# Folding a convolution through DRAM, moving products from VectorE to ScalarE and GpSimd, and a longer search for the instruction order

## The chip, the cores and the metric

The kernel runs on one core of a Trainium2 chip. The metric is device microseconds from start to end of one execution. Three executions of the kernel before took 842.36, 843.04 and 845.2 us; their median is 843.04 us. One further execution was recorded by the hardware profiler. Engines are called by the profile's names: PE is TensorE's matmul, PEld its weight load, DVE is VectorE, ACT is ScalarE, POOL is GpSimd, SP is SyncE (it issues DMAs).

## The reference

There are 4 batches. Each has an attention over 8 heads of 576 positions and 64 dimensions, in which every query keeps only its 32 largest scores, then two feed-forward blocks.

```python
scores = scale * np.matmul(q, k.transpose(0, 1, 3, 2))
kth = np.partition(scores, -32, axis=-1)[..., -32:-31]
scores = np.where(scores >= kth, scores, -1000000000.0)
attn = np.exp(scores - max);  attn = attn / (np.sum(attn) + 1e-09)
x = np.matmul(attn, v)                       # heads side by side: 576 x 512
# block 1
h = np.maximum(x @ w_in, 0.0);  u, v = h[..., :512], h[..., 512:]
v_n = (v - mean(v)) / np.sqrt(var(v) + 1e-06)
v_s = np.einsum('ts,bsd->btd', w_spatial, v_n) + b_spatial[None, :, None]
x = (u * v_s) @ w_out
# block 2: a causal convolution of 5 taps, each channel with its own taps
for k in range(5):
    gate_pre += conv_w[k][None, None, :] * xp[:, k:k + S, :]
out = ((1.0 / (1.0 + np.exp(-gate_pre))) * (x @ w_val)) @ w_out2
```

## The kernel before, in words

The work is cut into units. A unit is two tiles of 128 queries; a batch has 18 units, the program 72. For each unit PE makes the scores (`scores`, L475), ACT copies them from PSUM to the tile `sb` (L478), and DVE finds the 32nd largest of each row (`top`, L494 to L529): maxima and minima of halves and quarters give a list of candidates, and four rounds of an 8-fold maximum, with the found values replaced in between, walk down it. ACT takes the exponentials (L521). DVE multiplies them by the mask and sums them (`mask`, L546). ACT adds 1e-9 to the two sums (L550), DVE takes the reciprocal (L551), ACT scales the rows by it (L554). PE transposes them (L563, L568) and multiplies them by v (L584).

The two feed-forward blocks ("MoE") of batch b run beside the attention of batch b+1; those of batch 3 run alone after the last unit and are called the tail here. Their matrix products are kept near float32 by writing each operand as a high and a low part in the type fp32r and adding three products (`mm3`, L625). `hilo` (L604) makes the parts: ACT rounds the high part (L609), POOL subtracts it from the value for the low part (L611). In order, a batch has the pieces `piece_v` and `piece_u` (w_in), `piece_sp` (the product with w_spatial on PE, L728, then u times it on DVE, L733), `piece_x2` (w_out), `conv`, `piece_val` (w_val, then the gate times it on DVE, L805) and `piece_out`. Columns (positions) are worked in two halves of 288 and channels in four blocks of 128, so `piece_sp`, `conv` and `piece_val` each come 8 times a batch.

For batches 0 to 2 the convolution runs on PE: for each tap a 128x128 diagonal matrix of the coefficients, again in high and low parts, is multiplied with the shifted columns, 15 matmuls to a piece (L777). The 40 diagonals are built by ACT (L291). For batch 3 DVE does it by four multiply-adds a piece (L788). Since sigmoid(y) is (1 + tanh(y/2))/2, ACT makes the tanh (L780, L791) and DVE adds 1 while it multiplies by val (L805).

Weights come as 64-bit floats and are decoded at the start (`decode`, L305), written to DRAM and loaded again, 2 MB at a time, by DMAs that POOL issues (L403).

Nothing is issued in the order of the source. Every piece of work is recorded with its engine, an assumed duration and what it reads and writes (`Order.add`); `Order.play` then simulates a list schedule with these durations, and `Order.plan` plays it forward and back for 4 rounds and keeps the order with the shortest played time. That order is the program order of each engine, and each engine then issues strictly in that order: an instruction that waits holds up all that stand behind it on its engine.

Buffers that matter below: three PSUM banks `mp` for the MoE pieces while attention runs, three `sb`, two `e`, six `gate`.

## Time and profile before

| | before |
|---|---|
| median of three runs | 843.04 us |
| the profiled execution's own time | 839.99 us |
| its span, first to last instruction | 838.1 us |
| busy: PE, DVE, ACT, POOL | 708.3, 754.7, 602.8, 290.6 us |
| mean granted TensorE clock | 0.922 of full speed |

Busy time is the union of an engine's instructions; an instruction's duration includes a start and an end that overlap its neighbours, so in a dense stretch the time from one start to the next is what an instruction costs, and it is less than the mean that the profile prints. An fp32 matmul of the program (not a transpose, and not fp32r) is recorded as two. DVE's last instruction of attention ends at 742 us; the rest of the span is the tail.

### The profile page before, as it was taken

How to read it: one execution, taken by the hardware profiler on the slowest of the kernel's cores; microseconds unless marked ns; L12 is line 12 of the kernel's file. 1: busy time of each engine (PE TensorE's matmuls, PEld its weight loads, DVE VectorE, ACT ScalarE, POOL GpSimd, SP SyncE). 2: the span in 40 equal slices, each digit the busy share in tenths (PEclk: the TensorE clock that was granted, in tenths of full speed). 3: DMA queues.
4: the chain of work that ended last, by engine and by line, in shares of the span. 5: the costliest groups of instructions: out<-in, count | busy, mean ns of one | idle time of the engine just before them, and what ended most of it. 6: DMA issues, size and time to landing. Idle time of an engine off the chain costs nothing.

```text
span 838.1 us, 17270 instructions
## 1 busy us (share of the span) xinstructions
PE 708.3 (85%) x5969; PEld 605.2 (72%) x5969; DVE 754.7 (90%) x2749; ACT 602.8 (72%) x1390; POOL 290.6 (35%) x353
## 2 busy tenths in 40 slices
PE   3245545755899999998999999997999999999986
PEld 2234433544789899876888899875888999778985
DVE  6999999999999999999999999998989999951580
ACT  5668866777887777768977777786886777774341
POOL 4767255564523311132442322232333112322120
PEclk9955666777999999999999999998999999999999
DMA  7888332323134502153133412234035003533601
GB/s 248 245 261 304 101 121 91 115 86 109 39 100 146 184 2 76 55 196 120 29 134 113 156 30 102 100 101 143 2 142 194 23 2 131 210 120 123 221 2 61
DMA packets 46954, 99.25 MB, mean 118 GB/s; under 512 B 22532, under 2 KB 29960, under 8 KB 43272
## 3 DMA queue, kind: packets, MB, share of 16 engines
q0 software_dynamic: 4032, 53.74, 18.1%
q1 hardware_dynamic: 42824, 44.31, 16.8%
q8 instruction: 49, 0.80, 0.4%
q14 instruction: 49, 0.40, 0.2%
HBM read 79.88 MB, written 18.15 MB: 117 GB/s over the span
## 4 chain that ended last, share of the span: by engine, by line
DVE 51%; PE 23%; ACT 6%; issue 2%; POOL 1%; DMA 0%; POOLq 0%; DVEq 0%; ACTq 0%
DVE tw L527 10%; DVE e L546 10%; PE mp L625 8%; DVE t8b L529 7%; PE mp L728 4%; DVE tm L494 4%; DVE cand L503 4%; DVE tm L495 3%; DVE cand L506 3%; PE xr L584 3%; DVE t8a L516 2%; DVE cand L498 2%; PE sps L475 2%; DVE tn L499 2%; DVE gate L788 2%
## 5 line engine op out<-in xcount | busy, mean ns | idle before, releaser
L475 PE MATMUL sps<-k,q 64*128 64x144 f32 (+1 forms) x1280 | 126.4, 341 | 85.2 <-ACT sb L478 77.9
L475 PEld LDWEIGHTS sps<-k,q 64*128 64x128 f32 (+1 forms) x1280 | 90.4, 201 | 116.0 <-ACT sb L478 88.6
L546 DVE SCALAR_TENSOR_TENSOR e<-sb,t8b,e 128x576 f32<-128x576 f32 x144 | 132.5, 945 | 0.1
L529 DVE MAX8 t8b<-tw 128x8 f32<-128x168 f32 x432 | 120.3, 318 | 0.0
L554 ACT ACTIVATE e<-e,sums 128x576 f32<-128x576 f32 x144 | 106.6, 770 | 9.5 <-DVE sums L551 9.3
L521 ACT ACTIVATE e<-sb,neg 128x576 f32<-128x576 f32 x144 | 106.5, 770 | 2.2 <-PE ptp L563 1.0
L478 ACT ACTIVATE sb<-sps 128x576 f32<-128x576 f32 x144 | 93.0, 646 | 19.6 <-PE sps L475 17.2
L563 PE MATMUL ptp<-ident,e 128*128 128x128 f32 x576 | 94.5, 301 | 11.1 <-ACT e L554 8.5
L584 PE MATMUL xr<-pt,vt 128*64 128x128 f32 (+1 forms) x1280 | 87.8, 281 | 18.0 <-ACT pr L570 17.7
L625 PE MATMUL mp<-xh,wblk 128*128 128x288 f32 x448 | 102.2, 306 | 0.0
L584 PEld LDWEIGHTS xr<-pt,vt 128*64 128x64 f32 x1280 | 68.3, 144 | 36.4 <-ACT pr L570 23.6
L563 PEld LDWEIGHTS ptp<-ident,e 128*128 128x128 f32 x576 | 72.0, 153 | 25.0 <-ACT e L554 13.1
L527 DVE MATCH_REPLACE8 tw<-t8b,tw 128x168 f32<-128x168 f32 x288 | 88.8, 314 | 0.0
L565 ACT ACTIVATE pt<-ptp 128x512 f32<-128x512 f32 x144 | 81.7, 596 | 8.4 <-PE ptp L563 8.1
L625 PEld LDWEIGHTS mp<-xh,wblk 128*128 128x128 f32 x448 | 74.6, 188 | 5.5 <-issue 1.2
L625 PE MATMUL mp<-wblk,xh 128*128 128x512 f32 (+1 forms) x280 | 73.9, 406 | 1.1 <-POOL stage L327 1.1
L494 DVE TENSOR_TENSOR tm<-sb 128x576 f32<-128x576 f32 x72 | 58.8, 817 | 5.6 <-ACT sb L478 5.4
L611 POOL TENSOR_TENSOR yl<-ux,yh 128x288 fp32r<-128x288 f32 x31 | 29.5, 953 | 94.9 <-ACT yh L609 92.5
L625 PE MATMUL mp<-xl,wblk 128*128 128x288 f32 x224 | 60.9, 294 | 0.0
L625 PEld LDWEIGHTS mp<-wblk,xh 128*128 128x128 f32 (+1 forms) x280 | 49.8, 186 | 14.9 <-POOL stage L327 1.3
L495 DVE TENSOR_TENSOR tm<-sb 128x576 f32<-128x576 f32 x72 | 60.4, 838 | 0.0
L503 DVE MAX8 cand<-tm 128x8 f32<-128x288 f32 x144 | 57.8, 441 | 0.0
(180 smaller groups left out, 1687.9 us busy)
## 6 DMA issues: line engine op xcount, KB each, us to landing
wblk<-w_out POOLq DMA_DIRECT2D x7, 2048.0 KB, 8.4
wblk<-w_sp POOLq DMA_DIRECT2D x8, 1440.0 KB, 6.5
wblk<-w_inv POOLq DMA_DIRECT2D x4, 2048.0 KB, 8.3
wblk<-w_inu POOLq DMA_DIRECT2D x4, 2048.0 KB, 9.1
wblk<-w_val POOLq DMA_DIRECT2D x4, 2048.0 KB, 9.0
q<-in_qT SPq DMA_DIRECT2D x16, 288.0 KB, 3.9
k<-in_kT SPq DMA_DIRECT2D x16, 288.0 KB, 4.4
stage<-in_w_in SPq DMA_DIRECT2D x8, 512.0 KB, 4.5
```

Of the source, the lines that this page charges most:

```text
L475: nc.tensor.matmul(dst[:, f:f + QUART], lhsT=l, rhs=r[:, f:f + QUART], start=True, stop=True)
L478: od.add("ACT", t_actp(S), lambda c=c: nc.scalar.activation(sb[:, :, CH[c][0]:CH[c][1]], sps[:, :, 0:HALF], AF.Copy), [("sps",)], [("sb", ...
L494: tt(m[:, :, 0, :], sb[:, :, 0:HALF], sb[:, :, HALF:S], op=ALU.max)
L503: nc.vector.max(cand[:, t, QUART + 16:QUART + 24], m[:, t, 1, :])
L521: od.add("ACT", t_act(S, 1), lambda t=t: nc.scalar.activation(e[:, t, :], sb[:, t, :], AF.Exp, bias=neg[:, t:t + 1], scale=scale), ksb + [ ...
L527: nc.vector.match_replace(w[:, t, :], (t8a if r == 1 else t8b)[:, t, :], (src if r == 1 else w)[:, t, :], LOW)
L529: nc.vector.max(t8b[:, t, :], w[:, t, :])
L546: od.add("DVE", 0.85, lambda t=t, g=g: nc.vector.scalar_tensor_tensor(e[:, t, :], sb[:, t, :], t8b[:, t, 7:8], e[:, t, :], op0=ALU.is_ge, ...
L554: od.add("ACT", t_act(S, 1), lambda t=t, g=g: nc.scalar.activation(e[:, t, :], e[:, t, :], AF.Copy, scale=sums[:, g:g + 1]), [kg[t]], [("e ...
L563: nc.tensor.transpose(pp[:, j, :], e[:, t, REM * t + 128 * j:REM * t + 128 * j + 128], ident)
L584: nc.tensor.matmul(xr[64 * o:64 * o + 64, 2, 0:nq], lhsT=vt[:, kt, 64 * o:64 * o + 64], rhs=r, start=kt == 0, stop=kt == KT - 1)
L625: nc.tensor.matmul(ps, lhsT=l, rhs=r, start=m == 0, stop=m == len(ops) - 1)
```

## The change

1. **Convolution** (batches 0 to 2). `line_out` writes each finished x2 piece (128 channels by 288 columns and 4 more for the taps) to DRAM; four DMAs then read it back "folded" into one of three `fold` tiles: partition 32r+p holds channels p, 32+p, 64+p and 96+p, shifted by r columns. One matmul over the 128 partitions thus sums four taps of 32 channels, and a second one the fifth tap. For the four quarters of the channels that is 8 matmuls in plain fp32, each with 32 output partitions, in place of 15 with 128. Their weights, the tile `band`, are built by 4 POOL instructions after 14 small ACT ones; the 40 diagonals and the tile that held them are gone, and w_out of batch 3 gets a tile of its own (`wlate`) in the place of `band` and `fold`. The coefficients are loaded by 4 DMAs of 32 partitions and decoded at once (80 columns) and not in four jobs (5 columns).
2. **Products** of `piece_sp` and `piece_val` (batches 0 to 2): ACT copies PSUM to one of two `fac` tiles, POOL multiplies. ACT adds 1 to the gate in an instruction of its own.
3. **Sums**: 1e-9 is added on DVE, just ahead of the reciprocal.
4. **Order**: 200 rounds, with noise added to the order that is played back, and a score that is half the played time and half the mean time of three replays with durations lengthened at random by up to 20%. Assumed durations of POOL instructions and of two decode steps are changed as well.

```diff
-    ROUNDS = 4
+    ROUNDS = 200
+    SEED = 1
...
+        def score(run):
+            some = [self.replay(run[2], run[1], f) / 1.1 for f in factors]
+            return 0.5 * run[3] + 0.5 * sum(some) / len(some)
         best = run = self.play(own)
-        for _ in range(self.ROUNDS):
-            ends = [t + self.ops[i][0][e][0] for i, (t, e) in enumerate(zip(run[0], run[1]))]
-            late = self.play(lambda i, e: -ends[i] + (0.0 if first(i, e) else 1e4), back=True)
+        low = score(run)
+        for r in range(self.ROUNDS):
+            spread = 0.0 if r < 4 else rng.choice((0.0, 1.0, 3.0, 8.0))
+            ends = [t + self.ops[i][0][e][0] + spread * rng.gauss(0.0, 1.0) for i, (t, e) in enumerate(zip(run[0], run[1]))]
+            late = self.play(lambda i, e: -ends[i] + (0.0 if e == main[i] else 1e4), back=True)
             by = [late[3] - t - self.ops[i][0][e][0] for i, (t, e) in enumerate(zip(late[0], late[1]))]
-            run = self.play(lambda i, e: by[i] + (0.0 if first(i, e) else self.LATER))
-            best = min(best, run, key=lambda r: r[3])
+            run = self.play(lambda i, e: by[i] + (0.0 if e == main[i] else self.LATER))
+            now = score(run)
+            if now < low:
+                best, low = run, now
+            elif r >= 4:
+                run = best
...
+        NQR, NFOLD, FW = 4, 3, HALF + 1
...
-            flat = cw.rearrange("p k t -> p (k t)")
-            od.add("ACT", 0.2, lambda: nc.scalar.activation(cwp[0], flat, AF.Copy), [("cw",)], [("cwp", 0)], at)
-            od.add("POOL", 0.3, lambda: nc.gpsimd.tensor_tensor(cwp[1], flat, cwp[0].bitcast(F32), op=ALU.subtract),
-                   [("cw",), ("cwp", 0)], [("cwp", 1)], at)
-            for z in range(2):
-                part = cwp[z].bitcast(F32)
-                for d in range(KK):
-                    def go(z=z, d=d, part=part):
-                        for j in range(d * TAPS, (d + 1) * TAPS):
-                            nc.scalar.activation(DIAG[:, z, j, :], ident, AF.Copy, scale=part[:, j:j + 1])
-                    od.add("ACT", TAPS * 0.293, go, [("cwp", z)], [("diag", z, d)], at)
+            quarter = [slice(32 * r, 32 * r + 32) for r in range(4)]
+            def coefs():
+                nc.gpsimd.memset(coef, 0.0)
+                for r, rows in enumerate(quarter):
+                    nc.scalar.activation(cwn[rows], cw[rows, :, r, :], AF.Copy)
+                    nc.scalar.activation(ident4[rows, :], ident[rows, rows], AF.Copy)
+                    nc.scalar.activation(coef[rows, :, :, 0], cw[rows, :, :, r], AF.Copy)
+                nc.scalar.activation(coef[rows, :, :, 1], cw[rows, :, :, 4], AF.Copy)
+            od.add("ACT", 1.6, coefs, [("cw",)], [("cwn",), ("coef",)], at)
+            for d in range(KK):
+                def go(d=d):
+                    n = NQR * 2
+                    nc.gpsimd.tensor_tensor(
+                        BUF["band"][:, d].rearrange("p q m c -> p (q m) c"), ident4.unsqueeze(1).to_broadcast([128, n, 32]),
+                        coef[:, d].rearrange("p q m -> p (q m)").unsqueeze(2).to_broadcast([128, n, 32]), op=ALU.mult)
+                od.add("POOL", 0.8, go, [("coef",), ("cwn",), ("late",)], [("band", d)], at)
...
-            od.add("ACT", 0.2, lambda: nc.scalar.activation(sl, sl, AF.Copy, bias=1e-9), [], kg, ("r", at))
-            od.add("DVE", 0.07, lambda: nc.vector.reciprocal(sl, sl), [], kg, ("r", at))
+            def inverse():
+                nc.vector.tensor_scalar(sl, sl, 1e-9, None, op0=ALU.add)
+                nc.vector.reciprocal(sl, sl)
+            od.add("DVE", 0.135, inverse, [], kg, ("r", at))
...
+            def product(ps, j, x, kx, at):
+                fj = nxt(fa_n, NFAC)
+                od.add("ACT", t_actp(HALF), lambda: nc.scalar.activation(FAC[fj], ps[:, 0:HALF], AF.Copy), [("mp", j)], [("fac", fj)], at)
+                od.add("POOL", t_pool(HALF), lambda: nc.gpsimd.tensor_tensor(x(), x(), FAC[fj], op=ALU.mult) if callable(x) else
+                       nc.gpsimd.tensor_tensor(x, x, FAC[fj], op=ALU.mult), [("fac", fj)], kx, at)
...
                 g = UX[:, f, c0:c1]
-                od.add("DVE", t_dve(HALF), lambda: nc.vector.tensor_tensor(g, g, ps[:, 0:HALF], op=ALU.mult),
-                       [("mp", j)], kux(f, c0, c1), at)
+                if b < B - 1:
+                    product(ps, j, g, kux(f, c0, c1), at)
+                else:
+                    od.add("DVE", t_dve(HALF), lambda: nc.vector.tensor_tensor(g, g, ps[:, 0:HALF], op=ALU.mult),
+                           [("mp", j)], kux(f, c0, c1), at)
                 hilo(od, b, "x", f * XW + c0, f * XW + c1, lambda: g, kux(f, c0, c1), at)
...
+            def line_out(c, d, at):
+                c0, c1 = CH[c]
+                dj = LJ[c, d] = nxt(dr_n, len(sh.lines))
+                od.add("SP", fn=lambda: nc.sync.dma_start(sh.lines[dj], UX[:, d, c0:c1 + PADC]),
+                       r=kux(d, c0, c1 + PADC), w=[("lines", dj)], at=at, **dma(1, 512 * YW, 1.5))
...
+                    fj = nxt(fo_n, NFOLD)
+                    dj = LJ[c, d]
+                    lines = sh.lines[dj]
+                    def load():
+                        for r in range(4):
+                            nc.sync.dma_start(BUF["fold", fj][32 * r:32 * r + 32],
+                                              lines[:, r:r + FW].rearrange("(q p) s -> p q s", p=32))
+                    od.add("SP", fn=load, r=[("lines", dj), ("late",)], w=[("fold", fj)], at=at, **dma(4, 512 * NQR * FW, 1.5))
                     j = nxt(mp_n, banks)
                     ps = MP[j]
-                    ky = [k for r in region("y", d * YW + c0, d * YW + c1 + PADC) for k in r]
                     def go():
-                        ops = [(z, y, k) for k in range(TAPS) for z, y in ((0, "yh"), (0, "yl"), (1, "yh"))]
-                        ops.sort(key=lambda o: o[0])
-                        for m, (z, y, k) in enumerate(ops):
-                            nc.tensor.matmul(ps[:, 0:HALF], lhsT=DIAG[:, z, d * TAPS + k, :],
-                                             rhs=BUF[y][:, d * YW + c0 + k:d * YW + c1 + k], start=m == 0, stop=m == len(ops) - 1)
-                    od.add("PE", 15 * 0.143, go, ky + [("diag", z, d) for z in range(2)], [("mp", j)], at)
+                        for m in range(2):
+                            for q in range(NQR):
+                                nc.tensor.matmul(ps[32 * q:32 * q + 32, 0:HALF], lhsT=BUF["band"][:, d, q, m, :],
+                                                 rhs=BUF["fold", fj][:, q, m:m + HALF], start=m == 0, stop=m == 1)
+                    od.add("PE", 2 * 0.6, go, [("fold", fj), ("band", d)], [("mp", j)], at)
                     od.add("ACT", t_actp(HALF), lambda: nc.scalar.activation(acc(), ps[:, 0:HALF], AF.Tanh, scale=0.5),
                            [("mp", j), ("late",)], [("gate", gj)], at)
+                    od.add("ACT", t_act(HALF), lambda: nc.scalar.activation(acc(), acc(), AF.Copy, bias=1.0), [], [("gate", gj)], at)
...
                 gj = GJ[c, d]
-                od.add("DVE", t_dve(HALF), lambda: nc.vector.scalar_tensor_tensor(
-                    BUF["gate", gj], BUF["gate", gj], 1.0, ps[:, 0:HALF], op0=ALU.add, op1=ALU.mult), [("mp", j)], [("gate", gj)], at)
+                if b < B - 1:
+                    product(ps, j, lambda: BUF["gate", gj], [("gate", gj)], at)
+                else:
+                    od.add("DVE", t_dve(HALF), lambda: nc.vector.scalar_tensor_tensor(
+                        BUF["gate", gj], BUF["gate", gj], 1.0, ps[:, 0:HALF], op0=ALU.add, op1=ALU.mult), [("mp", j)], [("gate", gj)], at)
                 hilo(od, b, "x", d * XW + c0, d * XW + c1, lambda: BUF["gate", gj], [("gate", gj)], at)
...
-            for d in range(KK):
-                step(1.5, piece_x2, 0, d)
-                step(0, conv, 0, d)
-            for d in range(KK):
-                step(1.5, piece_x2, 1, d)
-                step(1.5, piece_val, 0, d)
-                step(0, conv, 1, d)
+            if b < B - 1:
+                for d in range(KK):
+                    step(1.5, piece_x2, 0, d)
+                    step(0, line_out, 0, d)
+                for d in range(KK):
+                    step(1.5, piece_x2, 1, d)
+                    step(0, line_out, 1, d)
+                    step(0, conv, 0, d)
+                for d in range(KK):
+                    step(1.5, piece_val, 0, d)
+                    step(0, conv, 1, d)
```

The first place is DVE's queue in the MoE of batch 1, at `piece_sp`. Names: `tw`, `t8b`, `cand`, `tm` belong to the search for the 32nd score, `e` and `sums` to the mask, `ux` is u, `mp` a PSUM bank. Before:

```order
L546 SCALAR_TENSOR_TENSOR e_100,sums<-sb_98,t8b,e_100 128x576
L527 MATCH_REPLACE tw<-t8a_109,cand 128x168 x2
L529 MAX t8b<-tw 128x8 x2
L551 RECIPROCAL sums<-sums 128x2
L527 MATCH_REPLACE tw<-t8b,tw 128x168 x2
L529 MAX t8b<-tw 128x8 x2
L733 TENSOR_TENSOR ux<-ux,mp_142 128x288
L527 MATCH_REPLACE tw<-t8b,tw 128x168 x2
L529 MAX t8b<-tw 128x8 x2
L733 TENSOR_TENSOR ux<-ux,mp_143 128x288
```

The same queue after, in the same batch; L605 is the mask, L611 the addition, L612 the reciprocal.

```order
L605 SCALAR_TENSOR_TENSOR e_109,sums<-sb_107,t8b,e_109 128x576 x2
L586 MATCH_REPLACE tw<-t8b,tw 128x168 x2
L588 MAX t8b<-tw 128x8 x2
L557 TENSOR_TENSOR cand<-tm 128x2x144
L558 TENSOR_TENSOR tn_124<-tm 128x288
L586 MATCH_REPLACE tw<-t8b,tw 128x168 x2
L588 MAX t8b<-tw 128x8 x2
L562 MAX cand<-tm 128x8 x2
L565 MAX cand<-tn_124 128x8 x4
L605 SCALAR_TENSOR_TENSOR e_108,sums<-sb_105,t8b,e_108 128x576 x2
L575 MAX t8a_117<-cand 128x8 x2
L611 TENSOR_SCALAR sums<-sums 128x2
```

The products have left DVE's queue, all 48 of batches 0 to 2, and before each of the 72 reciprocals stands an addition of DVE's own.

The second place is POOL's queue at `piece_sp` of batch 1, after (`fac` is the copy of the PSUM bank, L676 the low part, L456 the load of weights); before, L611 stands at L676's place and there is no product.

```order
L784 TENSOR_TENSOR ux<-ux,fac_153 128x288
L676 TENSOR_TENSOR xl<-ux,xh 128x288
L784 TENSOR_TENSOR ux<-ux,fac_154 128x288 x2
L676 TENSOR_TENSOR xl<-ux,xh 128x288
L456 DMA wblk_142<-w_out 128x4096
L784 TENSOR_TENSOR ux<-ux,fac_153 128x288
L676 TENSOR_TENSOR xl<-ux,xh 128x288 x2
```

The products now stand between low parts and weight loads on POOL, and ACT's copies into the two `fac` tiles wait for them.

The third place is PE's queue at a convolution. Before (batch 1; `diag` are the diagonals, `yh` and `yl` the parts of x2):

```order
L584 MATMUL xr<-pr_106,vt_92 64x128 x2
L777 MATMUL mp_143<-yh,diag 128x288
L777 MATMUL mp_143<-yl,diag 128x288
L777 MATMUL mp_143<-yh,diag 128x288
L777 MATMUL mp_143<-yl,diag 128x288
L777 MATMUL mp_143<-yh,diag 128x288
L777 MATMUL mp_143<-yl,diag 128x288
L777 MATMUL mp_143<-yh,diag 128x288
L777 MATMUL mp_143<-yl,diag 128x288
L777 MATMUL mp_143<-yh,diag 128x288
L777 MATMUL mp_143<-yl,diag 128x288
L777 MATMUL mp_143<-yh,diag 128x288 x5
```

After (batch 0; L690 are `mm3`'s matmuls for x2, L625 and L630 transposes, L534 scores, L866 the folded convolution):

```order
L690 MATMUL mp_150<-xh,wblk_141 128x288 x4
L625 MATMUL ptp_148<-ident,e_109 128x128 x4
L866 MATMUL mp_152<-fold_2046,band 32x288 x8
L625 MATMUL ptp_147<-ident,e_109 128x128 x4
L630 MATMUL xr<-ident,e_109 128x128
L866 MATMUL mp_150<-fold_2048,band 32x288 x8
```

A convolution that follows its x2 at once through ACT and POOL now follows a store and four loads that stand in SP's queue; scores and transposes stand right behind it in PE's. SP's queue at this place, after (`lines` is the DRAM copy):

```order
L840 DMA lines_71<-ux 128x292
L857 DMA fold_2046<-lines_70 32x4x289 x4
L857 DMA fold_2048<-lines_72 32x4x289 x4
L857 DMA fold_2047<-lines_71 32x4x289 x4
L840 DMA lines_73<-ux 128x292
L840 DMA lines_74<-ux 128x292
L840 DMA lines_75<-ux 128x292
L857 DMA fold_2046<-lines_73 32x4x289 x4
L857 DMA fold_2048<-lines_75 32x4x289 x4
```

There are 24 stores and 96 loads in all. The fourth load into a `fold` tile waits for the convolution that used the tile last.

## Rows read from the trace of the kernel before

**Rows 1.** Busy time by stretch (us, instructions in brackets), granted clock, DMA share.
```profile
core 0: us, PE busy (x) PEld busy (x) DVE busy (x) ACT busy (x) POOL busy (x), PEclk, DMA share, GB/s
240.00:740.00 500.00, 486.99 (x4328) 421.71 (x4327) 489.88 (x1893) 384.67 (x871) 138.06 (x179) 0.99 0.31 105
742.00:838.00 96.00, 85.55 (x579) 77.60 (x577) 37.88 (x78) 42.39 (x101) 19.01 (x36) 0.96 0.28 100
```

**Rows 2.** Waits, whole span: who waited for whom, us in total, times, longest.
```profile
ACT sums L550 <- DVE e L546: 23.8, 22, 3.5
DVE sums L551 <- ACT sums L550: 5.5, 7, 1.8
```

**Rows 3.** DVE's timeline at a product and at a reciprocal: start, us, instruction.
```profile
444.71 0.43 DVE L733 TENSOR_TENSOR ux<-ux,mp 128x288 f32<-128x288 f32 x1
445.06 0.08 DVE L527 MATCH_VALUE_LOAD tw<-t8b,tw 128x8 f32 x1
...
304.58 0.17 DVE L551 RECIPROCAL sums<-sums 128x2 f32<-128x2 f32 x1 [0.97 <-ACT sums L550]
304.66 0.07 DVE L527 MATCH_VALUE_LOAD tw<-t8b,tw 128x8 f32 x1
```

**Rows 4.** Groups by line: count, busy us, mean ns, idle before.
```profile
L546 DVE SCALAR_TENSOR_TENSOR e<-sb,t8b,e 128x576 f32<-128x576 f32 x144 | 132.5, 945 | 0.1
L495 DVE TENSOR_TENSOR tm<-sb 128x576 f32<-128x576 f32 x72 | 60.4, 838 | 0.0
L494 DVE TENSOR_TENSOR tm<-sb 128x576 f32<-128x576 f32 x72 | 58.8, 817 | 5.6 <-ACT sb L478 5.4
L611 POOL TENSOR_TENSOR yl<-ux,yh 128x288 fp32r<-128x288 f32 x31 | 29.5, 953 | 94.9 <-ACT yh L609 92.5 <-DVE yh L610 1.6 <-DVE tw L527 0.8
L780 ACT ACTIVATE gate<-mp 128x288 f32<-128x288 f32 x24 | 9.7, 405 | 9.4 <-PE mp L777 9.4
```

**Rows 5.** Single instructions by line: duration ns, minimum/median/maximum.
```profile
L546 DVE SCALAR_TENSOR_TENSOR e<-sb,t8b,e x144: 790/809/3159, 33.3 to 740.5; 128x576 f32<-128x576 f32 x144
L494 DVE TENSOR_TENSOR tm<-sb x72: 730/740/1861, 14.1 to 727.3; 128x576 f32<-128x576 f32 x72
L495 DVE TENSOR_TENSOR tm<-sb x72: 741/750/1826, 14.8 to 728.0; 128x576 f32<-128x576 f32 x72
```

**Rows 6.** Timeline of DVE and POOL from 305.5 us.
```profile
305.50 0.80 POOL L611 TENSOR_TENSOR yl<-ux,yh 128x288 fp32r<-128x288 f32 x1 [11.49 <-ACT yh L609]
305.74 1.18 DVE L494 TENSOR_TENSOR tm<-sb 128x576 f32<-128x576 f32 x1
```

**Rows 7.** PE's timeline: the products with v, a convolution, scores in two tile shapes.
```profile
300.07 0.76 PE L475 MATMUL sps<-k,q 64*128 64x144 f32 x8
300.76 0.40 PE L625 MATMUL mp<-xh,wblk 128*128 128x288 f32 x1
...
302.55 1.09 PE L584 MATMUL xr<-pt,vt 128*64 128x128 f32 x16
303.48 0.39 PE L584 MATMUL xr<-pr,vt 128*64 128x128 f32 x4
...
306.71 0.38 PE L777 MATMUL mp<-yh,diag 128*128 128x288 f32 x1
...
308.78 0.38 PE L563 MATMUL ptp<-ident,e 128*128 128x128 f32 x2
...
458.94 0.72 PE L475 MATMUL sps<-k,q 64*64 64x144 f32 x16
459.59 0.66 PE L563 MATMUL ptp<-ident,e 128*128 128x128 f32 x4
```

**Rows 8.** DMA issues: count, KB each, median us from issue to landing.
```profile
wblk<-w_val POOLq DMA_DIRECT2D x4, 2048.0 KB, 9.0
q<-in_qT SPq DMA_DIRECT2D x16, 288.0 KB, 3.9
out<-ost SPq DMA_DIRECT2D x16, 256.0 KB, 2.0
```

More of the change, by code (lines that the diff above doesn't have):

```diff
@@ L151, in play, with replay @@
         return start, taken, order, max(free.values())
+    def replay(self, order, taken, factor):
+        end, free = [0.0] * len(order), {}
+        for i in order:
+            e = taken[i]
+            ways, deps, lat = self.ops[i]
+            t = free.get(e, 0.0)
+            for d in deps:
+                g = taken[d]
+                t = max(t, end[d] + (self.SAME if g == e else self.SYNC).get(g, 0.0))
+            free[e] = t + ways[e][0] * factor[i]
+            end[i] = free[e] + lat
+        return max(free.values())
     def plan(self):
-        def first(i, e):
-            return e == next(iter(self.ops[i][0]))
+        rng = random.Random(self.SEED)
+        n = len(self.ops)
+        main = [next(iter(o[0])) for o in self.ops]
+        factors = [[1.0 + 0.2 * rng.random() for _ in range(n)] for _ in range(3)]
         def own(i, e):
@@ L404, in w_load, with w_load_late, go @@
                    [("scr", name)], [("wblk", j)], at, 9.0)
-        def w_load_late(od, name, at):
-            t = DIAG.rearrange("p z j c -> p (z j c)")
+        def w_load_late(od, name, scope, at):
+            t = [None]
             WT[name] = (t, ("wlate",))
-            od.add("POOL", 1.05, lambda: nc.gpsimd.dma_start(t[:, 0:WN[name]], sh.scratch[name]), [("scr", name)],
-                   [("wlate",)] + [("diag", z, d) for z in range(2) for d in range(KK)], at, 9.0)
+            def go():
+                scope.close()
+                t[0] = pool("wlate", 1, side="right").tile([128, WN[name]], F32R, name="wlate")
+                nc.gpsimd.dma_start(t[0], sh.scratch[name])
+            od.add("POOL", 1.05, go, [("scr", name)],
+                   [("wlate",)] + [("band", d) for d in range(KK)] + [("fold", j) for j in range(NFOLD)], at, 9.0)
         def wpart(t, lo):
             n = KK * FF
+            t = t[0] if isinstance(t, list) else t
             return t[:, lo * n:lo * n + n].rearrange("p (k f) -> p k f", k=KK)
@@ L916, in late_buffers @@
                     BUF[name, j] = p.tile([128, w], F32, name=f"{name}{j}")
+            p = conv_room.enter_context(tc.tile_pool(name="conv", bufs=1, side="right"))
+            BUF["band"] = p.tile([128, KK, NQR, 2, 32], F32, name="band")
+            for j in range(NFOLD):
+                BUF["fold", j] = p.tile([128, NQR, FW], F32, name=f"fold{j}")
         attention(od, 0, PER)
@@ L954, in attention_moe_kernel @@
         sh.again = keep.tile([1, 1], I32, name="again")
[L955 removed]
+        sh.conv = keep.tile([128, NP, 4, conv_w.shape[1]], F32, name="cw")
         half = S // 2
@@ L959, in attention_moe_kernel @@
                                    ("out", 4096), ("val", 4096), ("out2", 4096))}
+        sh.lines = [dram.tile([128, half + conv_w.shape[1] - 1], F32, name=f"lines{j}") for j in range(8)]
         attention_moe_pass(tc, sh, True, *args)
```

69 lines of the change are left out of this document (48 added, 21 removed).

## The prediction

> **What bounds the kernel now.** I read the stretches first, then DVE's waits, its groups, its timeline and PE's. Between 240 and 740 us, where attention and MoE run side by side, DVE is busy 489.88 of 500 us and PE 486.99; in the tail DVE is busy 37.88 of 96 us and PE 85.55 [rows 1]. Up to 742 us the end is therefore set by DVE's queue, with PE only 13 us of 500 behind it; after that by PE and the chain of batch 3, which the change leaves as it was but for the place of w_out. So whatever shortens DVE's queue before 742 us moves the tail forward by the same amount, as long as PE, ACT and the DMAs keep DVE fed. What DVE waits for itself is little: 5.5 us in 7 waits for the sums that ACT has added to [rows 2], and 5.4 us for `sb`, the idle time ahead of L494 [rows 4].
>
> **Products off DVE.** A product is recorded with 0.43 us, but the next instruction starts 0.35 us after it (444.71 to 445.06) [rows 3]. 48 go: 48 x 0.35 = 16.8 us less on DVE's queue. Nothing covers them there, since DVE has no gaps to speak of; I count them in full.
>
> **Sums on DVE.** The reciprocal of the same two elements costs 0.08 us from start to start (304.58 to 304.66) [rows 3]; the addition in front of it is taken at the same price: 72 x 0.08 = 5.8 us more. Below is no gain, above the recorded 0.17 us, 12.2 us, if the reciprocal cannot start until the addition has been written. In return the way DVE, ACT, DVE is gone, and with it the 5.5 us of waiting; ACT also loses 22 waits for the mask, 23.8 us, in which all behind it stood still [rows 2]. It will now stand at the scaling (L554) at most as long as the reciprocal is late.
>
> **Products on ACT and POOL.** ACT gets 48 copies out of PSUM and 24 additions to the gate, each priced as the tanh of the same shape, 0.405 us [rows 4]: 29 us, of which almost all falls into the 500 us in which ACT has 115 us idle [rows 1]; it loses 72 small additions there. I cost this at nothing for the end; the cover is ACT's idle time. If a copy waits, behind it on ACT stand the `sb` copies and the exponentials, for which DVE waits next. Each copy needs one of two `fac` tiles, so it waits when POOL is two products behind. POOL gets 48 products at the mean of its low parts of the same shape, 0.953 us [rows 4]: 45.7 us, with the four instructions for `band` some 49.5 us, in a stretch where it is busy 138 of 500 us [rows 1].
>
> **What POOL does to DVE.** This is the term that speaks against the change. A DVE instruction with two SBUF tensors takes 0.74 us when alone (median of L494) [rows 5]; the one at 305.74 shares 0.56 us with a subtraction on POOL and takes 1.18 us, 0.44 more [rows 6]. Over the run the means stand above the medians by 136 ns in 144 masks, 77 ns in 72 of L494 and 88 ns in 72 of L495 [rows 4, 5]: 19.6 + 5.5 + 6.3 = 31.4 us, against POOL's 290.6 busy us: 0.108 us of DVE for each us of POOL. 49.5 us more of POOL cost 5.4 us by that. From below: nothing, if they fall beside maxima and replacements. From above: the three groups fill 132.5 + 58.8 + 60.4 = 251.7 of DVE's 754.7 us, a third; if each meeting costs 0.44 of 0.56 us, 49.5 x 0.33 x 0.79 = 13 us. I take 7, near the average, since two shorter two-tensor groups are left out of it. The Trainium skill (GPSIMD Engine Reference, Specifications) says that GpSimd shares its SBUF interfaces with VectorE and that the two contend when a DVE instruction has two SBUF inputs. The trace agrees with 1.18 against 0.74 us; read as a full exclusion the rule gives the upper end, a forecast 6 us higher.
>
> **The convolution.** A piece costs PE 2.07 us now (306.71 to 308.78) [rows 7], 49.7 us for 24. Folded it is 8 fp32 matmuls, recorded as 16. No row has this shape. Products with v, fp32 with 64 output columns, need 0.93 us for 16 recorded ones with 128 moving columns [rows 7]; with 288 columns 2.09 us, so no gain at all, if tiles of 32 run no better than those of 64. But 16 score matmuls in 64x64 tiles take 0.65 us (458.94 to 459.59) where 8 in 64x128 tiles take 0.69 (300.07 to 300.76) [rows 7]: tiles of half the width run beside each other. By that four quarters lie side by side and the piece takes half, 1.05 us. I take this: 24 x 1.02 = 24.5 us less on PE. The Trainium skill (TensorEngine Tiling, Tiling Modes and Performance Considerations) agrees on four tiles of 128x32, and says against it that a change of tiling mode drains the array; by the first my 1.05 us stand, and no run here shows the price of the second. As DVE sets the pace, PE's 24.5 us count for nothing directly. They are room: with a stretch of 488 us PE needs 462.5. Of the 5.4 us that DVE waited for `sb`, which hung on PE and ACT, I take half as gone, 2.7 (between 0 and 5.4).
>
> A wait is added: PE now stands at the convolution until store and loads have landed, and behind it stand scores and transposes, so DVE starves once its three `sb` are used up. A store like that of an output takes 2.0 us, a load like q's 3.9 [rows 8]; in the order the first convolution of a batch has five other x2 pieces between its own x2 and itself, the later ones less, because the fourth load needs the first `fold` back. SP gets 120 DMAs in front of the loads of q, k and v, which come early by a good part of a batch; I cost that at nothing.
>
> **Search and small parts.** The diagonals' end on ACT, the loading of the coefficients at once and the better searched order I cost at nothing, between 3 us either way: DVE's stream has few gaps for an order to close, and the tail has the same pieces in nearly the same sequence.
>
> **Sum.** On the profiled execution: -16.8 (products) + 5.8 (additions) - 5.5 (wait for the sums) + 7 (POOL) - 2.7 (`sb`) = -12.2 us; 839.99 - 12.2 = 827.8 us. The median lies 3.05 us above the profiled execution, so I forecast 831 us.
>
> **Rivals.**
> *Nothing of it arrives.* If 32-wide tiles are no faster, a folded piece costs PE what it did, and PE with its 487 us and 13 us of waits keeps the stretch at 500 us: about 842 us. For it: PE is 97% busy. Against: the two shapes of scores.
> *The DMAs set the pace (slower).* PE waits in its queue at `fold`. For it: three `fold` tiles for 8 pieces, and weight loads of 2 MB that land after 9.0 us [rows 8] on the same DMA engines. Against: DMAs are busy 0.31 of the stretch [rows 1]. If a third of the 24 pieces meets such a load and comes 9.0 - 3.9 = 5.1 us late, PE stands 41 us; 25.3 us are room (487.8 - 462.5), 15.5 are not, and the time is 846.5 us. It decides from 37.5 us of standing on (25.3 + 12.2), 1.56 us for each piece.
> *All goes well.* POOL meets DVE where it does no harm, `sb` is never late: -16.8 + 5.8 - 5.5 - 5.4 = -21.9, about 821 us. For it: POOL's instructions are short and DVE has two tensors to read only a third of the time. Against: they met often enough so far.
>
> **How the numbers follow.** Forecast 0.60, with 824 to 838 as its own range (POOL at 0 and at 13 us); all goes well 0.15; nothing arrives 0.10; DMAs 0.15. The whole range, 818 to 846, reaches down past the best case by the 3 us of the order and up to the slower case. About 0.3%, 2.5 us, can be told from no change: faster 0.75, the same 0.11, slower 0.14.
>
> **What would show it.** Right: DVE's last reciprocal near 730 us and no line of PE's products in its queue; no DVE wait for sums; a folded piece near 1.05 us; the mean of the masks risen from 945 ns by some 30. Wrong: PE's wait at `fold` among its longest; DVE's wait for `sb` above 10 us; ACT standing at `fac`; DVE's groups of maxima, which share nothing with POOL, longer than before; a tail longer than 96 us.

## The result and the profile after

The changed kernel takes 853.79 us (median of 4 runs, 853.53 to 854.21) against 843.21 us (4 runs, 842.36 to 845.2) for the one before: ratio 1.0128 [1.0109, 1.0147], slower. The forecast was 831 us, faster. The profiled execution took 853.74 us with a span of 851.9 us.

The busy time by stretch answers to [rows 1]. The columns are the same.

```profile
core 0: us, PE busy (x) PEld busy (x) DVE busy (x) ACT busy (x) POOL busy (x), PEclk, DMA share, GB/s
240.00:740.00 500.00, 472.76 (x4406) 386.44 (x4407) 497.57 (x1873) 399.49 (x897) 190.80 (x237) 0.99 0.47 140
742.00:838.00 96.00, 89.30 (x608) 80.10 (x609) 50.13 (x128) 48.64 (x115) 20.64 (x40) 0.96 0.29 104
```

PE's busy time fell (487 to 473 us in the same 500, 708.3 to 699.5 us over the span), by less than the 24.5 us forecast, yet DVE is busier: 497.57 of 500 us, with 48 products fewer in its queue. The second row is no longer all tail, since the last reciprocal now ends at 754.9 us instead of 742.1. What follows it is 97.0 us, before 96.0. So the loss lies ahead of the last reciprocal, and on DVE. The groups and the single instructions by line, which answer to [rows 4] and [rows 5] (L605 is L546 of before, L553 and L554 are L494 and L495):

```profile
L605 DVE SCALAR_TENSOR_TENSOR e<-sb,t8b,e 128x576 f32<-128x576 f32 x144 | 135.9, 962 | 0.6 <-ACT e L580 0.6
...
L554 DVE TENSOR_TENSOR tm<-sb 128x576 f32<-128x576 f32 x72 | 63.3, 879 | 0.0
L553 DVE TENSOR_TENSOR tm<-sb 128x576 f32<-128x576 f32 x72 | 62.2, 863 | 0.0
...
L783 POOL TENSOR_TENSOR gate<-gate,fac 128x288 f32<-128x288 f32 x24 | 22.7, 946 | 51.0 <-ACT fac L782 50.8
L784 POOL TENSOR_TENSOR ux<-ux,fac 128x288 f32<-128x288 f32 x24 | 22.1, 927 | 33.2 <-ACT fac L782 24.2 <-issue 8.9
L611 DVE TENSOR_SCALAR sums<-sums 128x2 f32<-128x2 f32 x72 | 21.4, 297 | 0.0
```

```profile
L605 DVE SCALAR_TENSOR_TENSOR e<-sb,t8b,e x144: 794/818/1887, 28.5 to 753.7; 128x576 f32<-128x576 f32 x144
...
L611 DVE TENSOR_SCALAR sums<-sums x72: 144/167/1489, 40.3 to 754.5; 128x2 f32<-128x2 f32 x72
```

The last row of the groups is the surprise: the addition of 1e-9 to the two sums (a tile of 128x2, so two elements in each partition), for which the forecast had 5.8 us, is busy 21.4 us. Its median is 167 ns, its mean 297, its longest 1489. DVE's timeline at an undisturbed one:

```profile
315.44 0.15 DVE L611 TENSOR_SCALAR sums<-sums 128x2 f32<-128x2 f32 x1
315.62 0.17 DVE L612 RECIPROCAL sums<-sums 128x2 f32<-128x2 f32 x1
315.70 0.55 DVE L575 MAX8 t8a<-cand 128x8 f32<-128x168 f32 x2
```

and that of all engines at one that met POOL:

```profile
430.17 1.31 POOL L676 TENSOR_TENSOR yl<-vraw,yh 128x512 fp32r<-128x512 f32 x1 [8.23 <-ACT yh L674]
...
430.82 0.69 DVE L611 TENSOR_SCALAR sums<-sums 128x2 f32<-128x2 f32 x1
...
431.42 0.75 POOL L712 TENSOR_TENSOR xl<-xt,xh 128x256 fp32r<-128x256 f32 x1
431.54 0.17 DVE L612 RECIPROCAL sums<-sums 128x2 f32<-128x2 f32 x1
```

Undisturbed, 0.18 us pass from the addition's start to the reciprocal's, and 0.08 from the reciprocal's to the next. In the second, the addition is over when POOL's subtraction is (430.17 + 1.31 = 431.48 against 430.82 + 0.69 = 431.51). This is no single case: of the 27 additions that took more than 200 ns, 25 end 23 to 35 ns behind the end of an instruction of POOL. Over the 72, from the start of the addition to the next start on DVE: the 29 that ran without POOL at work took 0.19 us each, the 43 with it 0.43 on average, together 23.8 us.

All of DVE's queue up to the last reciprocal, added up from start to next start (idle time apart, so that 2.4 us of the 23.8 stand under idle; the two-tensor groups, whose instructions read two SBUF tensors, are mask, halves and quarters; e1 is the changed kernel without the addition):

```
us                         before   after      e1
products                     17.2     0.0     0.0
addition to the sums          0.0    21.4     0.0
reciprocals                   5.3     6.0     4.9
two-tensor groups           297.6   313.6   310.0
idle                         24.4    17.0    20.1
end of last reciprocal      742.1   754.9   735.5
```

The groups of maxima and replacements stayed as long as they were (the replacements 130.5 and 130.0 us). The waits, which answer to [rows 2], after, then two more of before, then the same two of e1:

```profile
ACT e L616 <- DVE sums L612: 37.3, 35, 5.5
ACT sb L537 <- DVE e L605: 26.2, 22, 2.5
```

```profile
PE ptp L625 <- ACT e L616: 41.0, 22, 8.0
```

```profile
ACT e L554 <- DVE sums L551: 9.3, 13, 1.3
...
PE ptp L563 <- ACT e L554: 8.5, 10, 2.0
```

```profile
PE ptp L624 <- ACT e L615: 30.2, 14, 8.3
...
ACT e L615 <- DVE sums L611: 20.9, 17, 4.3
```

DVE itself has no wait for sums. ACT had waited 23.8 us for the mask and 9.3 us for the reciprocal; now all of it is one wait of 37.3 us at the scaling, and PE waits behind it at the transposes. Without the addition (e1) 20.9 us of ACT's wait and 30.2 us of PE's are left, so most of PE's wait is not the addition's. A folded convolution on PE, and its DMAs:

```profile
L866 PE MATMUL mp<-fold,band x384: 402/406/431, 325.3 to 710.1; 128*32 128x288 f32 x192
```

```profile
fold<-lines SPq DMA_DIRECT2D x96, 144.5 KB, 4.0
```

From the start of a piece's first matmul to the start of the next instruction on PE it is 1.109 us (16 recorded ones; to the last one's end 1.18 us). In all PE's waits at `fold` come to 1.2 us.

### The profile page after: what moved, and what is told of

It is laid out like the page before. It is cut to its first block, busy times and chain, and to the rows that moved or that the text cites. A ratio compares the mean times of both kernels' runs of the same rounds, so it can differ in the third digit from the quotient of the medians.

```text
span 851.9 us, 17535 instructions
## 1 busy us (share of the span) xinstructions
PE 699.5 (82%) x5993; PEld 572.6 (67%) x5993; DVE 774.4 (91%) x2766; ACT 607.3 (71%) x1356; POOL 335.1 (39%) x400
## 4 chain that ended last, share of the span: by engine, by line
DVE 56%; PE 10%; ACT 4%; issue 2%; POOL 1%; POOLq 0%; ACTq 0%
DVE e L605 11%; DVE tw L586 10%; DVE t8b L588 7%; DVE tm L553 4%; DVE cand L562 4%; DVE tm L554 4%; PE mp L690 4%; DVE cand L565 3%; DVE t8a L575 3%; DVE tn L558 2%; DVE cand L557 2%; DVE gate L878 2%; DVE sums L611 1%; DVE sums L612 1%; PE sps L690 1%
## 5 line engine op out<-in xcount | busy, mean ns | idle before, releaser
L534 PE MATMUL sps<-k,q 64*128 64x144 f32 (+1 forms) x1280 | 127.1, 342 | 78.5 <-ACT sb L537 73.6
L534 PEld LDWEIGHTS sps<-k,q 64*128 64x128 f32 (+1 forms) x1280 | 91.1, 202 | 112.4 <-ACT sb L537 91.4
L605 DVE SCALAR_TENSOR_TENSOR e<-sb,t8b,e 128x576 f32<-128x576 f32 x144 | 135.9, 962 | 0.6 <-ACT e L580 0.6
L616 ACT ACTIVATE e<-e,sums 128x576 f32<-128x576 f32 x144 | 104.9, 770 | 38.1 <-DVE sums L612 37.3
L625 PE MATMUL ptp<-ident,e 128*128 128x128 f32 x576 | 97.8, 304 | 41.4 <-ACT e L616 41.0
L588 DVE MAX8 t8b<-tw 128x8 f32<-128x168 f32 x432 | 122.1, 327 | 0.0
L625 PEld LDWEIGHTS ptp<-ident,e 128*128 128x128 f32 x576 | 72.0, 154 | 58.3 <-ACT e L616 50.2
L646 PE MATMUL xr<-pt,vt 128*64 128x128 f32 (+1 forms) x1280 | 92.5, 289 | 17.4 <-ACT pt L627 10.6
L690 PE MATMUL mp<-xh,wblk 128*128 128x288 f32 x448 | 101.0, 305 | 0.6 <-ACT fac L782 0.4
L646 PEld LDWEIGHTS xr<-pt,vt 128*64 128x64 f32 x1280 | 71.9, 149 | 39.7 <-ACT pt L627 16.2
L690 PEld LDWEIGHTS mp<-xh,wblk 128*128 128x128 f32 x448 | 74.6, 189 | 6.3 <-issue 2.1
L690 PE MATMUL mp<-wblk,xh 128*128 128x512 f32 (+1 forms) x280 | 76.3, 416 | 0.0
L554 DVE TENSOR_TENSOR tm<-sb 128x576 f32<-128x576 f32 x72 | 63.3, 879 | 0.0
L553 DVE TENSOR_TENSOR tm<-sb 128x576 f32<-128x576 f32 x72 | 62.2, 863 | 0.0
L690 PE MATMUL mp<-xl,wblk 128*128 128x288 f32 x224 | 61.0, 295 | 0.0
L690 PEld LDWEIGHTS mp<-wblk,xh 128*128 128x128 f32 (+1 forms) x280 | 50.3, 189 | 14.7 <-issue 3.1
L690 PE MATMUL mp<-yh,wblk 128*128 128x288 f32 x232 | 53.5, 310 | 2.9 <-ACT yh L674 2.0
```

Of the source, the lines that this page charges most:

```text
L534: nc.tensor.matmul(dst[:, f:f + QUART], lhsT=l, rhs=r[:, f:f + QUART], start=True, stop=True)
L553: tt(m[:, :, 0, :], sb[:, :, 0:HALF], sb[:, :, HALF:S], op=ALU.max)
L554: tt(m[:, :, 1, :], sb[:, :, 0:HALF], sb[:, :, HALF:S], op=ALU.min)
L588: nc.vector.max(t8b[:, t, :], w[:, t, :])
L605: od.add("DVE", 0.85, lambda t=t, g=g: nc.vector.scalar_tensor_tensor(e[:, t, :], sb[:, t, :], t8b[:, t, 7:8], e[:, t, :], op0=ALU.is_ge, ...
L616: od.add("ACT", t_act(S, 1), lambda t=t, g=g: nc.scalar.activation(e[:, t, :], e[:, t, :], AF.Copy, scale=sums[:, g:g + 1]), [kg[t]], [("e ...
```

## Experiments

Theory A: the addition on DVE is what makes the kernel slower. Rival B: POOL's 48 products are, by what they do to DVE's two-tensor groups. Rival C: the searched order is. Later a third question: whether PE's 24.5 us were rightly counted as nothing. Ratios are against the kernel before on the same chip; a difference of ratios times 842.5 us, near the median of before, gives a difference of two experiments. By the intervals of the ratios such a difference is uncertain by 2 to 4 us. The runs without the addition leave 1e-9 out of the result.

**e1**, the changed order without the addition:

```
-                nc.vector.tensor_scalar(sl, sl, 1e-9, None, op0=ALU.add)
                 nc.vector.reciprocal(sl, sl)
```

> The changed kernel with every instruction at its place, but without VectorE's addition of 1e-9 ahead of the reciprocal (each sum contains exp(0) = 1, to which 1e-9 adds nothing in float32). Theory A, the addition is the loss: from the start of one addition to the next instruction 23.8 us pass in the changed kernel's 72 additions (0.33 us each, where I had put 0.08), so 853.8 - 23.8 = 830, at most 834. Rival B, GpSimd's products slow whatever VectorE does: VectorE then meets them elsewhere and the time stays above 848. Rival C, the searched order is at fault: above 848 as well.

Measured 834.08 us, 0.9904 [0.9869, 0.9939], at the upper end of what A gave. A holds, as B and C alone would have left the time above 848: one instruction of two elements, 72 times, is worth 0.0224 x 842.5 = 18.9 us, and without it the change is a gain.

**e3**, POOL's products on 8 of 288 columns (`x[:, 0:8]`, `FAC[fj][:, 0:8]`), the rest left out:

> The changed kernel, same order, with GpSimd's 48 products made on 8 of their 288 columns (the rest of the product is left out). GpSimd loses some 48 x 0.65 = 31 us. Theory B: the five two-tensor groups of VectorE lose the 15 us by which their time exceeds that of the kernel before, and the additions meet GpSimd less often: 834 to 840. If only the additions meet it (A): 5 us less, about 848. C: 853.

Measured 843.03 us, 1.0021 [0.9999, 1.0043]: between the ranges of B and of A. The two-tensor groups fall from 313.6 to 302.1 us, the additions only from 21.4 to 20.0. So POOL's products cost 9 us (0.0107) in this order, beside the addition, not instead of it.

**e4**, the products back on DVE, from `fac`, with everything else in place (`nc.gpsimd` to `nc.vector`):

> The changed kernel, same order, with the 48 products made by VectorE from the copies in fac, at the places where GpSimd made them. VectorE pays 48 x 0.36 = 17.3 us again. If a product on GpSimd costs VectorE about as much as it saves (B: 15 us in the two-tensor groups and some 4 in the additions), the time stays at 850 to 856. If the products on GpSimd are nearly free for VectorE, 866 or more.

Measured 861.81 us, 1.0265 [1.0222, 1.0309], between the two ranges expected: the move to POOL is worth 11.5 us net of what POOL does to DVE.

**e6**, the kernel before with ACT's addition left out (`lambda: None`):

> The kernel before, same order, without ScalarE's addition of 1e-9 to the sums. The round trip VectorE, ScalarE, VectorE goes: if it was worth what the prediction put down for it, 5.5 us less, 837 to 838; if ScalarE's 23.8 us of standing behind the mask also held up sb for VectorE, 832 to 836; if the waits come back elsewhere, 842 to 844.

Measured 837.86 us, 0.9946 [0.9917, 0.9975], as the first of the three expected.

**e2**, the addition as two instructions of one element:

```
-                nc.vector.tensor_scalar(sl, sl, 1e-9, None, op0=ALU.add)
+                for t in range(2):
+                    nc.vector.tensor_scalar(sl[:, t:t + 1], sl[:, t:t + 1], 1e-9, None, op0=ALU.add)
```

> The changed kernel, same order, with the addition made as two instructions of one element each. In the changed kernel an addition takes 0.195 us to the next start when GpSimd is idle and 0.49 when it is busy (33 of 72). Theory A1, the addition of two elements needs both of the ports that VectorE shares with GpSimd, and a single element does not: the meetings cost nothing, 33 x 0.3 = 10 us go, an instruction of 0.07 us is added, about 848. Rival A2, any addition on VectorE has to wait for GpSimd: two waits, 854 to 858.

Measured 847.09 us, 1.0053 [1.0031, 1.0075], 6.3 us faster than one instruction of two elements. Its line (duration in ns, minimum, median, maximum):

```profile
L612 DVE TENSOR_SCALAR sums<-sums x144: 123/136/150, 41.5 to 746.8; 128x1 f32<-128x1 f32 x144
```

None of 144 is longer than 150 ns; from start to start they take 0.114 us with POOL at work (95 of them) and 0.113 without. Waiting for POOL belongs to the form with two elements. (The expectation counted 33 meetings with POOL; the 43 above are all additions during which POOL was at work for any part.)

**e9**, the addition's result to a tile that nothing reads, the reciprocal in place as it was:

```
-                nc.vector.tensor_scalar(sl, sl, 1e-9, None, op0=ALU.add)
+                nc.vector.tensor_scalar(aside[:, 2 * u:2 * u + 2], sl, 1e-9, None, op0=ALU.add)
```

> The changed kernel, same order, with the addition's result written to a tile that nobody reads; the reciprocal reads the sums themselves (1e-9 is left out of the result). If the 0.195 us of an addition that meets nothing is the reciprocal's wait for its result, it falls to 0.08: 72 x 0.11 = 8 us less, about 845. If the instruction itself takes that long, no change, 853.

Measured 857.59 us, 1.0163 [1.0123, 1.0203], no faster than the changed kernel (the intervals overlap). The experiment did not do what was meant: undisturbed, the additions still take 0.18 us to the next start, because the reciprocal overwrites what the addition reads and so has to wait for it as before. **e13** takes that away too, with a tile `rec` for the reciprocal's result (the lines that make the tiles `aside` and `rec` are left out here):

```
-                nc.vector.tensor_scalar(sl, sl, 1e-9, None, op0=ALU.add)
-                nc.vector.reciprocal(sl, sl)
+                nc.vector.tensor_scalar(aside[:, 2 * u:2 * u + 2], sl, 1e-9, None, op0=ALU.add)
+                nc.vector.reciprocal(rec[:, 2 * u:2 * u + 2], sl)
...
-                    e[:, t, :], e[:, t, :], AF.Copy, scale=sums[:, g:g + 1]), ...
+                    e[:, t, :], e[:, t, :], AF.Copy, scale=rec[:, g:g + 1]), ...
```

> The changed kernel in its order; the addition's result goes to a tile that nothing reads, and the reciprocal goes from the sums into a tile of its own, by which ScalarE then scales (the 1e-9 is left out of the result), so that the reciprocal waits for no instruction of VectorE. Theory A (undisturbed, the addition's 0.195 us is mostly the reciprocal's wait for VectorE's own semaphore; about 0.115 us without it, as the one-element form showed): 72 x 0.08 = 6 us less than 853, so 845 to 849, with the 33 long ones behind GpSimd staying. Theory B (it is the two-element instruction itself): 852 to 855.

Measured 844.08 us, 1.0035 [1.002, 1.0049]: A, and slightly more of it, 7.8 us less than the changed kernel. DVE's timeline at an undisturbed one, and its line:

```profile
301.49 0.15 DVE L613 TENSOR_SCALAR aside<-sums 128x2 f32<-128x2 f32 x1
301.54 0.15 DVE L614 RECIPROCAL rec<-sums 128x2 f32<-128x2 f32 x1
301.62 0.80 DVE L607 SCALAR_TENSOR_TENSOR e<-sb,t8b,e 128x576 f32<-128x576 f32 x1
```

```profile
L613 DVE TENSOR_SCALAR aside<-sums x72: 137/158/1487, 41.6 to 745.1; 128x2 f32<-128x2 f32 x72
```

The reciprocal starts 0.05 us behind the addition, not 0.18: the 28 undisturbed ones take 0.06 us from start to start, before 0.19. The long ones stay (up to 1487 ns; the 44 with POOL at work take 0.34 us on average). Together the 72 take 16.6 us, where the changed kernel's take 23.8.

**e12**, the other way round: the kernel before in its order, with the addition moved from ACT to DVE and nothing else:

```
-            od.add("ACT", 0.2, lambda: nc.scalar.activation(sl, sl, AF.Copy, bias=1e-9), [], kg, ("r", at))
+            od.add("ACT", 0.2, lambda: None, [], kg, ("r", at))
...
+                nc.vector.tensor_scalar(sl, sl, 1e-9, None, op0=ALU.add)
                 nc.vector.reciprocal(sl, sl)
```

> The kernel before, same order, with the addition moved from ScalarE to VectorE as in the change, and nothing else. Without the addition it took 837.9 us. Theory A: 72 additions at 0.19 us are 14 us, and about a third of them meet GpSimd and lose 0.3 us, 7 us: 855 to 860, so this part of the change alone is slower than the kernel before. By my prediction (0.08 us each): 842 to 844.

Measured 847.09 us, 1.0061 [1.0036, 1.0086]. The forecast's gain from this part is refuted (it alone makes the kernel slower), but A's size is missed too: against e6 the addition costs 9.7 us, half of what it costs in the changed order. There are 23 additions with POOL at work instead of 43, and two-tensor groups and idle time gave some back (299.5 to 293.6 us, and 20.5 to 18.8).

**e5**, e1 with the products on DVE from `fac`; **e8**, e1 with 4 rounds of search instead of 200:

> The kernel without the addition (834.1 us), same order, with the 48 products made by VectorE from fac. With the addition in place this cost 9 us (861.8 against 852.7). If what GpSimd takes from VectorE lies mostly in the two-tensor groups, the same again: 841 to 845. If the additions were what GpSimd's products disturbed, the full 17 us come back: 849 to 852.

> The kernel without the addition (834.1 us) with 4 rounds of search, as before the change, and so with another order. If the search is worth nothing, 831 to 837; if it carries the gain, 840 or more.

e5 844.6 us, 1.0027 [1.0006, 1.0049]: the products' move is worth 10.4 us here. e8 839.27 us, 0.9954 [0.9931, 0.9977], between the two ranges expected: by the medians the search is worth 4.2 us on this program, but the intervals of e1 and e8 overlap.

**e7**, e1 with the 8 matmuls of each folded convolution twice; **e10**, e1 with the reciprocal alone in the plan (0.07 for 0.135), so with an order of its own; **e11**, e10 with the matmuls twice and planned so:

```
-                        for m in range(2):
+                        for m in (0, 1, 0, 1):
```

> The kernel without the addition (834.1 us), same order, with each folded convolution's 8 matmuls made twice into the same bank (the gate's argument is then doubled): 24 x 1.1 = 26.6 us more on PE, so PE has as much to do as in the kernel before. If VectorE sets the pace and what PE saves is only room, 834 to 838; if PE's saving carries the time, 845 or more.

> The kernel without the addition, its reciprocal put down with 0.07 us in place of 0.135, so the order is searched anew. If 834.1 us was no accident of one order, 829 to 838; below 831 if the right duration helps the order.

> The kernel without the addition and with each folded convolution's matmuls made twice (the gate's argument doubled), as in the run of 849.7 us, but with PE's time for it put down as 2.24 us, so the order is searched for it. If those 15.6 us were an order that did not know of them, 834 to 840; if PE's time is worth that in any order, 846 to 852.

e7 849.72 us, 1.0086 [1.0058, 1.0114]; e10 830.34 us, 0.9836 [0.9794, 0.9878]; e11 845.16 us, 1.0026 [1.0004, 1.0048], a little under the 846 to 852 expected. A doubled piece takes 2.08 us on PE and not twice 1.109, so the 24 pieces add 23.3 us, not the 26.6 expected. They make the kernel 15.3 us longer in a fixed order (e7 against e1) and 16.0 in a searched one (e11 against e10): PE's time is no room, about two thirds of it arrive. In e7 DVE's idle time up to the last reciprocal grew from 20.1 to 28.6 us. By the medians e10 is the fastest version, ahead of both kernels.

**e14, e15, e16** with e10 make a table of two by two under the same search, all without the addition: diagonal or folded convolution, products by DVE from PSUM or by ACT and POOL.

> The kernel before with the changed planner (200 rounds of disturbed play, the changed assumed costs) and without the addition of 1e-9 on any engine (left out of the result); diagonal convolution and VectorE's products stay. The kernel before without the addition took 837.9. Theory A (the search is worth the 4 to 5 us that 4 against 200 rounds gave): 833 to 835. Theory B (the search brings most of what the best version gains, and the two parts cancel): about 830. Theory C (the search brings nothing on this program): 837 to 839.

> The best version so far (folded convolution, no addition of 1e-9, own order, 830.3) with the products left to VectorE from the sums in PSUM. From the pair with the products on VectorE in a fixed order (8.6 to 10.5 us later): 838 to 841. If a new order makes up for it: 831 to 834. With the kernel below it says what the folding is worth beside VectorE's products: 15 us by the doubled convolution would put that kernel 15 us later than this one.

> The diagonal convolution with the products of three batches by ScalarE and GpSimd, no addition of 1e-9, changed planner: the best version so far without the folding. Theory A (TensorE's time is worth 15 us, as the doubled convolution showed): about 845. Theory B (TensorE's time is only room, and the doubled one lost for its order): 830 to 834. Theory C (the two parts add up from the kernel with neither): the time of that kernel less 9, so 824 to 829.

```
                      products by DVE                        products by ACT and POOL
diagonal convolution  e14 845.14, 1.0045 [1.0028, 1.0061]    e16 855.0,  1.0164 [1.0146, 1.0182]
folded convolution    e15 837.66, 0.9945 [0.9925, 0.9965]    e10 830.34, 0.9836 [0.9794, 0.9878]
```

In these four orders the two parts hang together. Products by POOL cost 10 us with the diagonals and bring 9.2 with the folding; the folding is worth 8.4 us beside DVE's products and 27.6 beside POOL's. e15 came out just below its first range; no range of e14 or e16 held the time (e14 was slower than any of its three, e16 by 10 us). The busy time up to and from 735 us, of e16 and then of e10:

```profile
240.00:735.00 495.00, 476.54 (x4280) 412.65 (x4276) 483.20 (x1823) 394.60 (x881) 175.60 (x224) 1.00 0.29 100
735.00:900.00 165.00, 102.13 (x667) 90.15 (x667) 52.49 (x124) 49.08 (x112) 25.62 (x44) 0.97 0.23 82
```

```profile
240.00:735.00 495.00, 472.77 (x4354) 388.17 (x4354) 479.45 (x1833) 396.55 (x889) 196.48 (x227) 0.98 0.47 142
735.00:900.00 165.00, 86.53 (x608) 78.39 (x607) 44.55 (x105) 44.79 (x105) 21.18 (x39) 0.98 0.17 61
```

In both, PE is busy some 475 of 495 us; what PE saves shows as 15.6 us less work left from 735 us on. e16's span is 20.3 us longer than e10's (851.3 and 831.0 us). Of these, 12.8 us come after the last reciprocal (103.3 and 90.5 us), where that work of PE is done, and 7.5 us before it (it ends at 748.0 and 740.5 us). Those 7.5 us are not waiting: DVE's idle time up to there is shorter in e16 (26.1 us) than in e10 (31.7 us), but the two-tensor groups take 312.6 against 298.8 us, with the same products on POOL. The longest wait of DVE for another engine in the attention, the decoding of the weights apart, in e16 and then in e10:

```profile
DVE tm L523 <- ACT sb L507: 11.4, 5, 5.1
```

```profile
DVE e L605 <- ACT e L580: 14.1, 2, 7.3
```

Every cell is one order, and an order has its own luck: e14 should have been e6 with a better search and is 8.3 us slower (0.0099). The two DVE instructions of `bits`, a step of decoding the weights, take 9.3 us more (38.2 us against 28.9 up to the last reciprocal), since they fall on POOL's work more often in this order (22.9 us of overlap against 10.0); smaller differences go both ways. With e6 in e14's place the table would say that the folding is worth nothing beside DVE's products and that POOL's products cost 18 us with the diagonals.

## Why the prediction was wrong

**The step that failed** is "Sums on DVE", the price of the addition. "The addition in front of it is taken at the same price" as the reciprocal: 5.8 us, with 12.2 as the upper end. It measured 23.8 us. By e13, 72 x 0.06 = 4.3 us of it are the instruction, near the 5.8; 72 x 0.13 = 9.4 us the reciprocal's wait for an instruction of its own engine; 43 x (0.43 - 0.19) = 10.3 us waits for POOL (together 24.0, rounded). The border between the last two is not sharp: e13, which takes the wait for the own engine away, keeps 16.6 us, so that by it the two are 7.2 and 12.3 us. The first two lie near the upper end that the step itself gave; the third was in no bound, because POOL's harm was reckoned for instructions with two tensors only. Taken away, the addition makes the kernel 18.9 us faster (e1) and turns the sign. The Trainium skill (SBUF — State Buffer, Who interferes with whom) says that a `tensor_scalar` can enter a mode with two ports, and that then whichever of it and a GpSimd instruction issues first holds the shared pair of ports to its end. The Trainium skill (VectorE: DVE Perf Modes, Mode 2×_2P) says that this mode splits the outermost dimension longer than one between the ports, which a single element doesn't have. The rows agree: up to 1489 ns with two elements, at most 150 with one, and 25 of the 27 long ones ended with an instruction of POOL. No run shows the mode itself.

**The way DVE, ACT, DVE.** Right for DVE: its wait for the sums is gone. Wrong for ACT: its waits for the mask, 23.8 us, were booked as lost, but they only moved to the scaling, where ACT already stood 9.3 us. It stands there for 37.3 us, against 33.1 in both places before; e1, without the addition, has 20.9. PE's wait behind it grew from 8.5 to 41.0 us, of which e1 keeps 30.2, so that most of this growth comes with the order and not with the addition.

**Products off DVE.** Right: 17.2 us are gone, forecast 16.8.

**POOL's harm to DVE.** Too small: 7 us, bounds 0 and 13; the two-tensor groups grew by 16.0 us, 11.5 of which go with POOL's full products (e3), and the masks' mean by 17 ns only, since halves and quarters took most. The average of before, 0.108 us for each us of POOL, was no fair price here, and no fixed price is: with the same products on POOL the two-tensor groups take 310.0 us in e1's order and 298.8 in e10's, where before they took 297.6.

**The convolution.** Its price was right, 1.109 us for 1.05, and PE doesn't stand at `fold` (1.2 us), so the slower rival by DMAs did not happen. "PE's 24.5 us count for nothing directly" was wrong. [Rows 1] had both engines at 97 to 98% of the stretch, and I took DVE alone for the bound. e7 and e11 show that about two thirds of PE's time arrive at the end, in the fixed order and in the searched one; by the table of four the folding is worth from 8.4 to 27.6 us by what stands beside it. This error has the other sign; without it the forecast would have missed by more.

**The wait for `sb` and the search.** Idle time fell by 7.4 us, forecast 8.2 with the wait for the sums; DVE's wait for `sb` is gone, and ACT stood only 1.2 us for a free `fac`. The search brought 4.2 us in e8, a little over the 3 allowed, and in e14 a loss.

**Together.** Against before, DVE's end moved by 12.8 us: -17.2 (products) + 21.4 (addition) + 0.7 (reciprocals) + 16.0 (two tensors) - 7.4 (idle) + 2.2 (decoding) leave 15.7; -2.9 is spread over the rest. "Decoding" here is `bits` alone. That the change would be slower was given 0.14, for another reason.

What stays open: how much of the 27.6 us is the folding's and how much the luck of two orders, and so how large the interplay in the table is; several seeds for each cell were not run. Open too is why PE's busy time fell by only 8.8 us over the span when the convolution alone, at 1.109 for 2.07 us a piece, gives 23.

## What to carry to other kernels

An instruction of two elements is not priced by its size: look whether the next one on its engine needs its result (0.13 us here) and whether it is of a form that waits for GpSimd (up to 1.49 us here). When two engines are both near 97% of a stretch, relieving one alone brought 8 us or lost 10, relieving both brought 18 (against e14; against e6, another order of the same program, nothing, a loss of 18 and a gain of 9): price the pair, not the one with the higher figure, and allow for the order, which alone made 8 us between e14 and e6. Before a small operation is moved to the engine that sets the pace, time it there alone, undisturbed and disturbed.

## What the runs showed of the hardware

- A VectorE `tensor_scalar` of 128x2 elements takes 0.06 us of the queue when nothing behind it has to wait for it (e13), 0.19 when the next instruction does, and up to 1.49 us in the changed kernel and 2.29 us in e12 when GpSimd is at work; 25 of the 27 that took over 200 ns ended 23 to 35 ns behind a GpSimd instruction. As 128x1 it took at most 150 ns in 144 cases, 95 of them with GpSimd at work. The reciprocal of 128x2 elements took at most 181 ns in any run.
- Four quarters of the array, 128x32 each, ran side by side in fp32: 16 recorded matmuls with 288 columns in 1.109 us, at 406 ns each. In a piece at 327.08 us four start within 20 ns and the next four 0.27 us after the first.
